# The second batch's X loads behind the third DMA transpose, and eight more identity products at the start

## The chip, the cores and the metric

The kernel runs on one core of a Trainium2 chip. The metric is the device time of one execution in microseconds (us). The engines are TensorE (PE; its weight loads are shown apart as PEld), VectorE (DVE), ScalarE (ACT), GpSimd (POOL) and SyncE (SP). SP computes nothing here: it issues DMAs, in order, and waits in front of a DMA whose source is not ready.

## The reference

One block of a speech encoder, for two batches of 4000 rows of 144 values. Cut to its core:

```
h = layernorm(x);  x = x + 0.5 * (silu(h @ w_ff1a) @ w_ff1b)       # 144 -> 576 -> 144
h = layernorm(x);  q, k, v = split(h @ w_qkv)                      # 4 heads of 36
x = x + softmax(q k^T * 36**-0.5) v @ w_o                          # all 4000 keys of the batch
h = layernorm(x);  a, b = split(h @ w_pw1);  h = a * sigmoid(b)
x = x + silu(depthwise_conv5(h, dw)) @ w_pw2
h = layernorm(x);  x = x + 0.5 * (silu(h @ w_ff2a) @ w_ff2b)
return layernorm(x)
```

## The kernel before

Rows are worked on in 16 chunks of 500, eight for each batch (CPB = 8, NCH = 16). A chunk lies in the tile X as 125 partitions by 4 blocks of 144 values. Each chunk passes two norms ahead of attention (feed-forward 1, then Q, K and V), and three after it.

A norm takes its statistics on DVE (`bn_stats`, tile ST, two instructions for a chunk), the root on POOL (tile RS), and writes normed rows into XN, on DVE, ACT or POOL. The matmuls that follow want the 144 values along the partitions, in two halves of 72. There are two ways to turn the rows:

- The first chunks of the opening (`small(c)`, chunks 0 to 3) go through PE: a product with the identity matrix (PS<-IDENT,XN in the profile) and a copy out of PSUM into XTB or XTQ.
- Later chunks go through a DMA transpose that SP issues, `dma_transp`, line 1201: XTB<-XN. For the attention norm two plain DMAs, XTQ<-XTB, follow it.

In the feed-forward part PE multiplies XTB by WA (and its remainder WE), ACT applies tanh (TH<-PS), DVE makes HT from TH and PS, and PE multiplies HT by WB. In attention PE computes scores (PS<-QT,KT), ACT or DVE their exponentials (PT<-PS), and PE multiplies these by V (PS<-PT,VA).

The kernel's text is run by a planner: every operation becomes a record with its engine, its cost and what it depends on. The planner groups the records into steps, one for each value of `R.step`. A table, ORDER, then says for each engine in which order the steps are issued, and `arrange` puts them so; two characters of a table name one step of that engine. From the records come the semaphore waits. All DMAs of SP go through one hardware queue (q1 in the profile), in SP's order.

The inputs are loaded thus: X of chunk 0 and of chunks 1 to 7 by SP, the first feed-forward weights and the QKV weights by ACT, then on SP the other weights and, in the same step as the last of them, the eight X loads of the second batch (`load_x`, 140.6 KB each). The first DMA transpose comes next on SP.

At the start PE has no rows yet. `warm` gives it products of the identity matrix by itself (PS<-IDENT, 128x128), 50 of them (NWARM) ahead of the first rows. Their result is not used. The same products also fill some gaps later on (`R.filler`).

Of the kernel before, what the change touches and what calls it, by code (L numbers as in the profile page):

```python
# [12 lines left out]
D = 144  # L13
H = 4
# [183 lines left out]
        ')o*/*#*$*)**)r*&*(*+*1*-*2*4*3*5*6*0*,*7*8'  # L198
    ),
    "pool": (  # L200
        '!!!#!$!%!&!+!(!)!*!,!-!1!B!@!/!2!4!3!.!0!5!8!9!A!:!=!6!?!<!;!7!>!D!C!E!}!G!F!J!H!I!K!L!N!t!M!O!Q!T!k'
        '!P!R!Y!S#3!U!j!W!V!`!X!Z![!]!^!f!h!_!a!b!d!g!i!c!e!l!m!n!o!u!v!w!p!y!x!z!{!r!q!|#$#!!s#&###)#(#*#%#/'
        '#1#0#2#+#-#,#.#5#6#7#8#4#;#<#=#>#Z#?#D#@#:#A#F#E#9#B#C#G#J#H#I#O#K#Q#L#M#N#S#T#P#U#V#W#X#R#^#Y#[#]#`'
        '#_#a#b#t#c#f#j#h#i#e#d#k#p#r#m#q#n#o#g#l#s#v#x#w#y#u#z$&#{#|#}$!$$$#$%$($)$*$+$,$-$/$.$0$1$2$3$4$5$6'
        '$7$>$<$=$G$?$B$@$:$A$C$E$8$D$F$M$I$K$9$H$J$N$L$;$O$Q$P$R$Y$S$W$T$X$U$[$]$Z$V$^$`$b$e$a$_$c$f$g$h$i$d'
        '$j$l$n$o$u$p$q$k$m$s$r$t$v$x$z$w%($|$y%#%!%$${%%%&%)$}%*%,%-%.%/%0%+%1%2%9%3%4%5%6%=%>%?%;%7%B%<%C%8'
        '%D%E%F%:%G%@%J%A%M%H%I%K%L'
    ),
    "sp": (
        '!!!#!$!%!&!(!)!*!+!,!-!.!/!0!1!2!4!3!5!6!8!9!;!7!<!=!>!?!A!:!@!C!D!E!F!B!G!H!I!J!K!N!P!M!L!Q!O!R!U!S'  # L210
        '!T!V!W!X!Z!Y![!_!]!^!`!d!a!e!f!g!b!h!l!i!c!j!n!m!k!o!p!q!s!t!u!r!x!v!{!y!|!z!w!}###!#$#%#&#*#(#)'
    ),
}
PLACES = (
# [92 lines left out]
def c_dve(n, rate=1.0):  # L307
    return n / (960 * rate) + 0.07
# [456 lines left out]
def bass_standalone__conformer_family_zipformer__speech_kernel(  # L765
# [13 lines left out]
    Bsz, T, Dm = x.shape  # L779
    assert Dm == D and T % CH == 0  # L780
    N = Bsz * T
# [8 lines left out]
    R = Rec(nc)  # L790
    op = R.op
    S = Sched(R)

    def sb(name, shape, dt=BF16):
        return nc.alloc_sbuf_tensor(name, [128] + list(shape), dt)
# [150 lines left out]
    ROT = 0  # L946
    SPLIT = 0
    NWARM = 50
    NPRE = 3
    KEEP = 2  # L950
    ALONE = 3
# [15 lines left out]
    X = sb("X", [NBLK, D])  # L967
# [47 lines left out]
    BX = 6  # L1015
# [22 lines left out]
    def load(eng, q, dst, src, w, r=(), lat=None):  # L1038
        op(eng, "dma_start", dst, src, q=q, r=r, w=w, cost=0.45, lat=lat)

    def kh(wap):
        return wap.rearrange("(k p) n -> p k n", p=HD)

    def load_x(eng, c, r=()):
        load(eng, f"x{c}", X[0:TB, c * NB:(c + 1) * NB, :], x_tok[c], [("X", c, i) for i in range(NB)], r, 2.9)

    def load_ff(eng, qa, qb, WA, WE, WB, wa, wb, nm, la=None, lb=None):
        load(eng, qa, WA[0:HD, :, :], kh(wa)[:, :, 0:512], [(nm, "a", 0)], lat=la)
        load(eng, qa, WE[0:HD, :, 64:128], kh(wa)[:, :, 512:FF], [(nm, "a", 1)], lat=la)
        load(eng, qb, WB[:, 0:4, :], wb[0:512, :].rearrange("(t p) d -> p t d", p=128), [(nm, "b", 0)], lat=lb)  # L1050
        load(eng, qb, WB[0:64, 4, :], wb[512:FF, :], [(nm, "b", 1)], lat=lb)
        load(eng, qb, WB[64:128, 5, :], wb[512:FF, :], [(nm, "b", 2)], lat=lb)
# [28 lines left out]
        load("sp", "w2", WP2Z[i * LC:(i + 1) * LC, i, :], w_pw2[ML:D, :], [("WP2Z", i)])  # L1081
    load("sp", "w2", DWR[0:KCONV, 0:D], dw, ["DWR"])
    load_ff("sp", "w2", "w2", WA2, WE2, WB2, w_ff2a, w_ff2b, "W2")
    for c in range(CPB, NCH):
        load_x("sp", c)

# [22 lines left out]
    def warm(cost=0.056, bk=BX + 1, n0=0):  # L1109
        op("pe", "matmul", PSV[:, bk, n0:n0 + 128], lhsT=IDENT[:, :], rhs=IDENT[:, :], start=True, stop=True, r=["ID"],  # L1110
           w=[("ps", bk)], cost=cost, kind="f")

    for i in range(NWARM):
        warm(0.1, BX + i % 2, i // 2 % 4 * 128)
    R.filler = warm
    R.filler_free = lambda: max([o.done for h in R.hist[("ps", BX + 1)] for o in h if o.eng != "pe"], default=0.0) + 0.06

# [493 lines left out]
    def pre(c):  # L1611
        if c == 0:
            yield from pre_first()
        else:
            yield from ff1(c)
            yield from pre2(c)
# [282 lines left out]
    def series(gens):  # L1899
        for g in gens:  # L1900
            yield from g
            if ROT:
                S.threads.remove(S.cur)
                S.threads.append(S.cur)
# [216 lines left out]
    for c in range(CPB):  # L2121
# [3 lines left out]
                m=c_dve(2 * CH, 2), w=c_dve(2 * CH, 4))  # L2125
# [161 lines left out]
    def pick():  # L2287
        got = pick_any()
        if mode["front"] and not stats["exp"] and not (got[1] == "T" and got[2].rank < 0):
            eng = "pe" if got[1] in "SO" else got[2].req.eng if got[1] == "T" else "act"  # L2290
            ts = [(S.start_of(th), th) for th in S.threads if th.rank < 0 and th.req.eng == eng]
            ts = [q for q in ts if q[0] is not None and q[0] < max(got[0], R.free[eng]) + FIRST]
            if ts:
                t, th = min(ts, key=lambda q: q[0] - 0.25 * q[1].req.hold + FJ[q[1].no % len(FJ)])
                return t, "T", th
        return got
# [98 lines left out]
    while n_s[0] < NIT or eq or pend or live_dve[0]:  # L2395
        seg[0] = max(seg[0], n_s[0] // SEG)
        if mode["front"] and len(kv_done) == CPB:
            mode["front"] = False
            front[:] = [0.0, n_s[0]]
            S.add(setup_dw())  # L2400
            for par in range(NPRE):
                S.add(series(pre(c) for c in range(CPB + par, NCH, NPRE)), R.last)
            for par in range(2):
# [3 lines left out]
        if due():  # L2407
            n = n_s[0]
# [13 lines left out]
        t, k, v = pick()  # L2422
        R.step += 1
        if k == "S":
            n = n_s[0]
# [15 lines left out]
    while S.threads:  # L2441
        c = [(S.start_of(th), th) for th in S.threads]
        c = [(t, th) for t, th in c if t is not None]
# [42 lines left out]
```

## Time and profile before

| | us |
|---|---|
| median of 3 runs | 880.66 |
| the three runs | 879.81, 880.66, 881.91 |
| the profiled execution | 877.03 |
| its span, first to last instruction | 875.2 |
| PE / DVE / ACT / POOL busy | 854.3 / 843.8 / 838.6 / 282.8 |

The span is 1.8 us shorter than the time of the same execution. All rows of the profile are from that execution, and their times count from the start of its span. Nearly every instruction is recorded by one helper and shows line L591, so groups are told apart by engine and tile. A row of a timeline merges neighbouring instructions of one kind (x8 is eight of them); its second number runs from the first one's start to the last one's end. For SPq that is the time of issuing, not of the transfer.

### The profile page before, as it was taken

The page shows a single profiled execution, that of the slowest core. Times are in us where ns is not written, and L with a number is a line of the kernel's source. Part 1 is how long each engine was busy: PE and PEld are TensorE (multiplying, and loading weights), DVE is VectorE, ACT ScalarE, POOL GpSimd, SP SyncE. Part 2 cuts the span into 40 slices and gives each one's busy share as a digit, 9 for nine tenths or more (in the row PEclk, how much of TensorE's full clock was granted, in tenths as well). Part 3 has the DMA queues.
Part 4 walks back from the last instruction along what each step waited for, and adds up shares of the span by engine and source line. Part 5 has one row for each costly group of instructions (what it writes and reads, how often), then busy time and mean ns, then how long its engine had stood idle before and what let it go on. Part 6 is the DMA issues. An engine that isn't in the chain of part 4 may idle for free.

```text
span 875.2 us, 27133 instructions
## 1 busy us (share of the span) xinstructions
PE 854.3 (98%) x11629; PEld 412.5 (47%) x11629; DVE 843.8 (96%) x1853; ACT 838.6 (96%) x1101; POOL 282.8 (32%) x540
## 2 busy tenths in 40 slices
PE   8999999999999999999999999999999999999996
PEld 7643444444344444444444444444545444444586
DVE  7899999999999999999999999999999999999987
ACT  7799999999999999999999999999999999999975
POOL 6670341031514302511330241210541261501645
PEclk9999999999999999999999999999999999999999
DMA  4420111102122101211310010201120021010201
GB/s 120 71 45 8 32 21 38 32 15 44 21 38 39 38 15 20 44 26 26 33 37 2 9 37 9 26 13 14 26 51 4 19 44 26 17 18 14 41 20 40
DMA packets 83552, 26.12 MB, mean 30 GB/s; under 512 B 78231, under 2 KB 83432, under 8 KB 83432
## 3 DMA queue, kind: packets, MB, share of 16 engines
q1 hardware_dynamic: 81884, 23.70, 14.8%
q8 instruction: 91, 1.49, 0.7%
q10 hardware_dynamic: 1548, 0.69, 0.3%
q14 instruction: 29, 0.24, 0.1%
HBM read 3.31 MB, written 2.30 MB: 6 GB/s over the span
## 4 chain that ended last, share of the span: by engine, by line
ACT 44%; PE 36%; DVE 16%; DMA 2%; issue 1%; POOL 1%; DVEq 0%; POOLq 0%; ACTq 0%
ACT PT L591 40%; PE PS L591 36%; DVE PT L591 10%; ACT TH L591 3%; DMA XTB<-XN 2%; DVE ST L591 1%; DVE X L591 1%; DVE U L591 1%; DVE XN L591 1%; DVE QT L591 0%; DVE HT L591 0%; DMA X<-in_x_dram 0%; DVE KT L591 0%; POOL RS L591 0%; POOL XN L591 0%
## 5 line engine op out<-in xcount | busy, mean ns | idle before, releaser
L591 ACT ACTIVATE PT<-PS 128x1000 bf16<-128x1000 f32 (+1 forms) x793 | 731.8, 1075 | 7.0 <-PE PS L591 5.5
L591 PE MATMUL PS<-QT,KT 64*64 64x500 bf16 x3968 | 455.8, 383 | 4.3 <-ACT PT L591 1.0
L591 PE MATMUL PS<-PT,VA 64*37 64x500 bf16 x4828 | 451.8, 372 | 1.8 <-DVE QT L591 0.9
L591 DVE TENSOR_SCALAR PT<-PS 128x500 int16<-128x500 f32 (+1 forms) x424 | 280.8, 680 | 4.5 <-PE PS L591 2.4
L591 PEld LDWEIGHTS PS<-QT,KT 64*64 64x64 bf16 x3968 | 138.6, 104 | 203.8 <-ACT PT L591 102.6
L591 PEld LDWEIGHTS PS<-PT,VA 64*37 64x37 bf16 x4828 | 162.9, 96 | 106.9 <-DVE PT L591 15.1
L591 POOL TENSOR_SCALAR RS<-ST 125x4 f32<-125x4 f32 (+1 forms) x118 | 31.1, 265 | 485.4 <-DVE ST L591 481.0
L591 DVE TENSOR_SCALAR PT<-PT 128x1000 uint16<-128x1000 uint16 x430 | 172.3, 418 | 1.7 <-PE PS L591 0.5
L591 DVE TENSOR_TENSOR PT<-PT 128x1000 bf16<-128x1000 bf16 x215 | 146.0, 682 | 1.1
L591 POOL TENSOR_SCALAR XN<-X,RS 125x144 bf16<-125x144 bf16 x236 | 134.6, 582 | 3.9 <-DMA out_dram<-XN 0.3
L591 POOL TENSOR_TENSOR RS<-RS,NHALF 125x4 f32<-125x4 f32 (+2 forms) x99 | 97.0, 983 | 71.8 <-DVE RS L591 69.5
L591 ACT ACTIVATE TH<-PS 128x500 bf16<-128x500 f32 (+3 forms) x175 | 95.0, 568 | 5.2 <-PE PS L591 4.5
L591 PE MATMUL PS<-XTB,WA 72*128 72x500 bf16 (+2 forms) x304 | 72.5, 344 | 3.1 <-DMA XTB<-XN 2.5
L591 DVE SCALAR_TENSOR_TENSOR HT<-TH,PS 128x500 bf16<-128x500 bf16 (+1 forms) x120 | 72.0, 617 | 3.4 <-ACT TH L591 2.4
L591 DVE BATCH_NORM_STATS2 ST<-X 125x6 f32<-125x288 bf16 (+1 forms) x160 | 66.4, 450 | 2.1 <-DMA X<-in_x_dram 1.2
L591 DVE SCALAR_TENSOR_TENSOR X<-PS,X 125x288 bf16<-125x288 f32 (+1 forms) x112 | 50.2, 452 | 4.6 <-PE PS L591 3.7
L591 PE MATMUL PS<-WB,HT 128*125 128x144 bf16 (+1 forms) x640 | 51.9, 229 | 0.1
L591 PEld LDWEIGHTS PS<-WB,HT 128*125 128x125 bf16 (+1 forms) x640 | 44.8, 136 | 12.6 <-issue 3.6
L591 PEld LDWEIGHTS PS<-XTB,WA 72*128 72x128 bf16 x304 | 22.9, 97 | 30.5 <-issue 9.0
L591 PE MATMUL PS<-U,DG 128*128 128x375 bf16 (+5 forms) x204 | 27.9, 263 | 0.1
L591 ACT ACTIVATE HT<-PS 128x500 bf16<-128x500 f32 (+3 forms) x46 | 21.4, 526 | 4.1 <-PE PS L591 3.6
L591 PE MATMUL PS<-IDF,QT 128*125 128x128 f32 x128 | 22.4, 298 | 0.0
(95 smaller groups left out, 523.0 us busy)
## 6 DMA issues: line engine op xcount, KB each, us to landing
X<-in_x_dram SPq DMA_DIRECT2D x16, 140.6 KB
XTQ<-XTB SPq DMA_DIRECT2D x24, 70.3 KB
out_dram<-XN SPq DMA_DIRECT2D x11, 140.6 KB
XTB<-XN SPq DMA_TRANSPOSE x50, 3.0
out_dram<-XN SPq DMA_DIRECT2D x6, 70.3 KB
XTB<-AN SPq DMA_TRANSPOSE x15, 3.1
out_dram<-XN ACTq DMA_DIRECT2D x3, 70.3 KB
WA<-in_w_ff1a_dram ACTq DMA_DIRECT2D x1, 144.0 KB
```

What stands on the lines that cost most here:

```text
L591: ins = getattr(eng, o.name)(*o.a, **o.k)
```

## The change

Two edits, and new order tables that number the steps anew.

- A step of their own for the eight X loads of the second batch. In SP's table this step is put behind the third DMA transpose. Before, SP issues: weights, eight X loads, four transposes. After: weights, three transposes, eight X loads, the fourth transpose.
- Eight more identity products (NMORE) behind the 50. The planner's clocks are put back to where they were ahead of them, so that they change nothing in what it plans.

On every engine the order of all else is the same, and no instruction gets a wait that it did not have.

```diff
     "sp": (
-        '!!!#!$!%!&!(!)!*!+!,!-!.!/!0!1!2!4!3!5!6!8!9!;!7!<!=!>!?!A!:!@!C!D!E!F!B!G!H!I!J!K!N!P!M!L!Q!O!R!U!S'
...
+        '!!!#!%!&!(!$!)!*!+!,!-!.!/!0!1!2!3!5!4!6!7!9!:!<!8!=!>!?!@!B!;!A!D!E!F!G!C!H!I!J!K!L!O!Q!N!M!R!P!S!V'
...
     NWARM = 50
+    NMORE = 8
...
     load_ff("sp", "w2", "w2", WA2, WE2, WB2, w_ff2a, w_ff2b, "W2")
+    R.step += 1
     for c in range(CPB, NCH):
         load_x("sp", c)
...
     def warm(cost=0.056, bk=BX + 1, n0=0):
         op("pe", "matmul", PSV[:, bk, n0:n0 + 128], lhsT=IDENT[:, :], rhs=IDENT[:, :], start=True, stop=True, r=["ID"],
            w=[("ps", bk)], cost=cost, kind="f")
+        return R.ops[-1]
 
     for i in range(NWARM):
         warm(0.1, BX + i % 2, i // 2 % 4 * 128)
+    was = dict(R.free), R.last, R.issue, list(R.quad), R.kind
+    for i in range(NMORE):
+        R.trims.append((warm(0.056, BX + i % 2, i // 2 % 4 * 128), 0.056, 0.1))
+    R.free, R.last, R.issue, R.quad, R.kind = was
```

The table of POOL changes too, only because the steps after the new one have other numbers.

More of the change, by code (lines that the diff above doesn't have):

```diff
@@ L200 @@
     "pool": (
[L201 to L207, printed above, removed]
+        '!!!#!$!%!&!(!,!)!*!+!-!.!2!C!A!0!3!5!4!/!1!6!9!:!B!;!>!7!@!=!<!8!?!E!D!F#!!H!G!K!I!J!L!M!O!u!N!P!R!U'
+        '!l!Q!S!Z!T#4!V!k!X!W!a!Y![!]!^!_!g!i!`!b!c!e!h!j!d!f!m!n!o!p!v!w!x!q!z!y!{!|!s!r!}#%##!t#(#$#*#)#+#&'
+        '#0#2#1#3#,#.#-#/#6#7#8#9#5#<#=#>#?#[#@#E#A#;#B#G#F#:#C#D#H#K#I#J#P#L#R#M#N#O#T#U#Q#V#W#X#Y#S#_#Z#]#^'
+        '#a#`#b#c#u#d#g#k#i#j#f#e#l#q#s#n#r#o#p#h#m#t#w#y#x#z#v#{$(#|#}$!$#$%$$$&$)$*$+$,$-$.$0$/$1$2$3$4$5$6'
+        '$7$8$?$=$>$H$@$C$A$;$B$D$F$9$E$G$N$J$L$:$I$K$O$M$<$P$R$Q$S$Z$T$X$U$Y$V$]$^$[$W$_$a$c$f$b$`$d$g$h$i$j'
+        '$e$k$m$o$p$v$q$r$l$n$t$s$u$w$y${$x%)$}$z%$%#%%$|%&%(%*%!%+%-%.%/%0%1%,%2%3%:%4%5%6%7%>%?%@%<%8%C%=%D'
+        '%9%E%F%G%;%H%A%K%B%N%I%J%L%M'
     ),
     "sp": (
-        '!!!#!$!%!&!(!)!*!+!,!-!.!/!0!1!2!4!3!5!6!8!9!;!7!<!=!>!?!A!:!@!C!D!E!F!B!G!H!I!J!K!N!P!M!L!Q!O!R!U!S'
-        '!T!V!W!X!Z!Y![!_!]!^!`!d!a!e!f!g!b!h!l!i!c!j!n!m!k!o!p!q!s!t!u!r!x!v!{!y!|!z!w!}###!#$#%#&#*#(#)'
+        '!!!#!%!&!(!$!)!*!+!,!-!.!/!0!1!2!3!5!4!6!7!9!:!<!8!=!>!?!@!B!;!A!D!E!F!G!C!H!I!J!K!L!O!Q!N!M!R!P!S!V'
+        '!T!U!W!X!Y![!Z!]!`!^!_!a!e!b!f!g!h!c!i!m!j!d!k!o!n!l!p!q!r!t!u!v!s!y!w!|!z!}!{!x#!#$###%#&#(#+#)#*'
     ),
```

## The prediction

> **What bounds the kernel now.** I read the page first, for the balance of the engines.
>
> ```profile
> span 875.2 us, 27133 instructions
> PE 854.3 (98%) x11629; PEld 412.5 (47%) x11629; DVE 843.8 (96%) x1853; ACT 838.6 (96%) x1101; POOL 282.8 (32%) x540
> ```
>
> Three engines are busy for 96 to 98% of the span, in an order that is written out, so a stall in the opening stage pushes everything behind it, and only there is anything left to gain. The change touches nothing but the first microseconds of PE and one stretch of SP's queue. So the chain of waits between 20 and 55 us comes next (start, length, what).
>
> ```profile
> 23.04 0.27 DVE XN L591
> 23.30 6.31 DMA XTB<-XN
> 29.62 0.05 issue
> 29.66 17.16 PE PS L591 x192
> 46.83 0.02 issue
> 46.85 1.00 ACT PT L591
> ```
>
> The first DMA transpose is a link of that chain: 6.31 us, then 17 us of matmuls without a break, then the attention stage. SP's timeline shows what stands ahead of it, and the list of DMA issues what a transpose usually takes (its last number, from issue to landing).
>
> ```profile
> 16.42 4.81 SPq L591 DMA_DIRECT2D X<-in_x_dram  x8
> 23.30 8.98 SPq L591 DMA_TRANSPOSE XTB<-XN  x2
> 35.71 1.23 SPq L591 DMA_TRANSPOSE XTB<-XN  x1
> 51.55 1.23 SPq L591 DMA_TRANSPOSE XTB<-XN  x1
> XTB<-XN SPq DMA_TRANSPOSE x50, 3.0
> X<-in_x_dram SPq DMA_DIRECT2D x16, 140.6 KB
> ```
>
> So it took 3.3 us longer than the usual 3.0. The eight X loads were all issued by 21.23, so SP was not what held the transpose; the data was. The DMA view between 20 and 40 us, in 40 slices of half a microsecond, shows it:
>
> ```profile
> DMA  3334333339933333860000004992000001993000
> GB/s 122 118 124 150 124 120 124 124 118 256 175 124 120 124 124 99 160 150 0 0 0 0 0 0 99 216 198 61 0 0 0 0 0 32 219 206 67 0 0 0
> ```
>
> A stream of about 122 GB/s runs from before 20 to about 28 us: the X loads (8 of 140.6 KB, 1.15 MB, 9.4 us at that rate). The transpose appears in two pieces, in slices 10 and 11 (24.5 to 25.5) and, when the stream ends, in slices 17 and 18 (28 to 29). The second transpose (32 to 34) and the third (36.5 to 38.5), with nothing beside them, are one piece each of under 2 us. The first is half done and then waits for the X loads.
>
> **The X loads behind the third transpose.** What the stall costs, engine by engine (timelines; in brackets the idle time before and its releaser):
>
> ```profile
> 26.64 1.44 PE L591 MATMUL PS<-XTB,WA 72*128 72x500 bf16 x6
> 29.66 0.60 PE L591 MATMUL PS<-XTB,WA 72*128 72x500 bf16 x2 [1.59 <-DMA XTB<-XN]
> 26.61 2.19 ACT L591 ACTIVATE TH<-PS 128x500 bf16<-128x500 f32 x4 [0.18 <-PE PS L591]
> 30.73 1.97 ACT L591 ACTIVATE TH<-PS 128x250 bf16<-128x250 f32 x4 [1.92 <-PE PS L591]
> 27.38 2.41 DVE L591 SCALAR_TENSOR_TENSOR HT<-TH,PS 128x500 bf16<-128x500 bf16 x4
> 31.14 0.42 DVE L591 SCALAR_TENSOR_TENSOR HT<-TH,PS 128x250 bf16<-128x250 bf16 x1 [1.34 <-ACT TH L591]
> 35.68 1.59 DVE L591 SCALAR_TENSOR_TENSOR HT<-TH,PS 128x500 bf16<-128x500 bf16 x3 [0.31 <-ACT TH L591]
> 21.42 1.85 POOL L591 TENSOR_SCALAR XN<-X,RS 125x144 bf16<-125x144 bf16 x4
> ```
>
> When is the first transpose issued? It waits for POOL, which finishes its rows at 21.42 + 1.85 = 23.27; that is unchanged, and SP, now free since 16.4, issues at 23.30 as before. With nothing ahead it lands at 23.30 + 3.0 = 26.30. What is late next is PE itself: from its rows of six and of two such matmuls a further one costs (1.44 - 0.60)/4 = 0.21 us, so the one that waits could start at 26.64 + 6 x 0.21 = 27.90, not 29.66: 1.76 earlier. The landing is then 1.6 us early, so it need not be exact. ACT is free at 28.80 and could gain up to 1.92; it follows PE. DVE is free at 29.79 and can move its next HT by only 1.34 at first. These three bound the gain, 1.34 to 1.92. I take 1.75, nearest to PE's row, because the 17.16 us behind it are a chain of PE, and DVE, 0.41 short at first, has 0.31 of idle time at 35.68 to catch up in.
>
> Then everything up to the end would move by 1.75, if nothing with a fixed time stands in the way. The next such items are the second and third transposes, and the first consumers of both on PE's load row:
>
> ```profile
> 29.23 1.79 POOL L591 TENSOR_SCALAR XN<-X,RS 125x144 bf16<-125x144 bf16 x4
> 33.01 2.67 POOL L591 TENSOR_SCALAR XN<-X,RS 125x144 bf16<-125x144 bf16 x6
> 37.69 0.58 PEld L591 LDWEIGHTS PS<-XTB,WA 72*128 72x128 bf16 x4
> 42.82 0.20 PEld L591 LDWEIGHTS PS<-XTB,WA 72*128 72x128 bf16 x2
> ```
>
> POOL, not moved by the change, ends their rows at 31.02 and 35.68, and SP issues at 31.05 (the second of the row of two: 23.30 + 8.98 - 1.24) and 35.71. They land at about 34.1 and 38.7. Their consumers, moved forward by 1.75, come at 35.94 and 41.07. Margins: 1.8 and 2.4 us. So neither stalls, provided that the third is not slowed.
>
> The eight loads themselves now start at 35.71 + 1.23 = 36.94 and hold SP for 4.81 us, to 41.75. Behind them on SP stands the fourth transpose, which waits for rows that come with the moved chain, at 51.55 - 1.75 = 49.80: 8 us after SP is free. Their data takes 9.4 us after a start-up; even with 2 us of that it has drained by 48.4, so 1.4 us are left. Who needs the X of the second batch?
>
> ```profile
> L591 DVE BATCH_NORM_STATS2 ST<-X x28: 435/448/463, 4.7 to 51.6; 125x6 f32<-125x288 bf16 x28
> 91.03 0.81 DVE L591 BATCH_NORM_STATS2 ST<-X 125x6 f32<-125x288 bf16 x2
> ```
>
> The first row is that of the tile ST up to 90 us. The first batch alone has eight chunks with two norms of two such instructions ahead of attention, 32 in all, so the 28 started by 51.6 fit into it, and the next comes at 91.03. Loads that land by 48.4 are 42 us early. Cost of the delay: nothing. Removed from 17 to 28 us is DMA traffic that no other row waits for.
>
> **Eight more identity products.** They stand behind the 50 at the start of PE's queue, with no wait of their own. The rows:
>
> ```profile
> 1.52 4.60 PE L591 MATMUL PS<-IDENT 128*128 128x128 bf16 x50 [1.52 <-POOL NHALF L591]
> 6.76 0.41 PE L591 MATMUL PS<-IDENT,XN 125*72 125x125 bf16 x4 [0.65 <-DVE XN L591]
> L591 PE MATMUL PS<-IDENT x33: 260/314/314, 1.5 to 4.9; 128*128 128x128 bf16 x33
> 10.73 0.55 PE L591 MATMUL PS<-IDENT 128*128 128x128 bf16 x7
> 11.89 0.89 PE L591 MATMUL PS<-IDENT 128*128 128x128 bf16 x13
> ```
>
> The first 33 start within 1.5 to 4.9 us, 3.4/32 = 0.106 us apart; later ones, by the rows of 13 and of 7, (0.89 - 0.55)/6 = 0.057. So here the clock doubles at about 5 us. Eight at 0.057 are 0.46 us, inside the 0.65 that PE waits for DVE's first rows: nothing on the path. If the clock were still slow, the 50 would end their starts at 1.52 + 50 x 0.106 = 6.82, already behind 6.76, and eight at 0.106 would put 0.85 us in front of the first rows. These are the bounds, nothing and 0.85; I take nothing, since the row shows the fast pitch. A gain from them (a clock that is released sooner) has no row: the release comes before they run.
>
> The Trainium skill (TensorE: Matmul & The Clock Gate, Part 1) says that the clock is released by a free-running activity window of about 3.4 us, so that the moment differs between runs. By that rule this trace (release about 3.4 us after the first product) has nearly the earliest moment, other executions pay up to the whole 0.85, and the sum would be a gain of about 0.9. One trace cannot show the spread.
>
> **The sum.** Gain 1.75 - 0 = 1.75 us. The profiled execution took 877.03 us for its span of 875.22; it would become 875.3, with a span of 873.5. The median of the runs is 880.66, 3.6 above the profiled execution, and they range from 879.81 to 881.91. I take the same difference off the median: 878.9. The bound for a difference that a measurement of this kernel can tell, 0.2%, is 1.76 us, so the forecast lies on that bound.
>
> **Rivals.**
>
> *The clock comes later.* The eight products then stand ahead of the first rows. Price: up to 0.85, deciding from the point where 58 products end after 6.76, which is a release about 0.7 us later than here (the 0.65 idle less 0.46 leaves 0.19; each microsecond of slow clock costs 0.5). Against it: the pitch in the trace. It leaves a gain of 0.9 to 1.7, or 879.0 to 879.8. I put into this case, too, that the gain is given back later to some transfer whose margin I have not seen.
>
> *The stall is longer in the timed runs.* They are 3.6 us longer than the profiled execution. If some of that is a slower X stream, the wait for the first transpose is longer by as much, and the change removes all of it: at one to two more microseconds, 877 to 878. Against it: the stream in the trace is steady at 122 GB/s.
>
> *The third transpose is caught (slower).* The first one was held half done until the X stream ended. If loads issued right behind a transpose, in the same queue, can hold it too, the third lands at the end of the drain, some 48.4 + 0.5 us, rather than 38.7. PE then waits at the weights that begin at 42.82 now, and the time grows by about 6: 887. It decides from a landing after 42.82 + 1.76 = 44.6; between 41.07 and 42.82 it only eats the gain. For it: the first transpose shows that a transpose beside X traffic can stand still. Against it: there the loads were ahead, issued from 16.42, and the third is finished by 38.5 while loads issued at 36.94 have hardly begun to move data. The change also is what it says: in the built order only the eight loads and the products move, and no wait is added.
>
> **The numbers.** Forecast 0.58, of which about half falls on either side of the bound (0.30 faster, 0.28 same), given the scatter of about 1 us in the runs; longer stall 0.20 (faster); late clock or gain given back 0.13 (same); third transpose caught 0.09 (slower). So 0.50, 0.41 and 0.09. The forecast's own range is 878.2 to 879.6 (1.34 to 1.92, and the scatter of a median); with the longer stall below, and a lost gain and scatter above, 877.4 to 881.0, which leaves out the slower case and a tenth more.
>
> **What would show it.** In the profile after: the eight X loads of SP at about 37; the first transpose still issued at 23.3 and landing 3 us later; PE's wait of 1.59 before the matmul at 29.66 gone, that matmul at 27.9; matmuls of the third transpose at about 41.1 without a wait for DMA; the attention stage, at 46.85 now, at 45.1; PE's first rows still at 6.76, with a gap of 0.2. I am wrong if the first transpose still takes over 4.5 us, if XTB appears as a releaser around 41 us, or if the first rows come after 6.9.

## The result and the profile after

| | before | after |
|---|---|---|
| median, us | 880.23 (10 runs) | 875.26 (10 runs) |
| lowest and highest | 876.65 and 882.88 | 874.88 and 875.96 |
| profiled execution: time, span | 877.03, 875.2 | 875.88, 874.0 |

The ratio is 0.9951, with a 95% interval of 0.9931 to 0.9970: faster by 5 us, where 1.75 was forecast, and outside the range given. Two numbers of the table matter more than the medians. The two profiled executions differ by 1.15 us only. And the runs of before spread over 6 us, those of after over one. Sorted, the ten runs of before are 876.65, 876.85, 877.28, 877.39, and then 879.81 to 882.88: two groups, and the profile on which the prediction rests came from the lower one.

What the change does in its own stage is what was forecast. SP's timeline after:

```profile
23.45 13.69 SPq L591 DMA_TRANSPOSE XTB<-XN  x3
37.19 4.67 SPq L591 DMA_DIRECT2D X<-in_x_dram  x8
```

The DMA view after, from 20 to 50 us in 40 slices of 0.75 us:

```profile
DMA  1000006900000000493000198133334333333200
GB/s 22 0 0 0 0 0 139 202 9 0 0 11 0 0 0 22 97 184 80 0 0 0 37 214 157 51 108 123 121 121 145 120 121 123 123 123 121 100 0 0
```

The first transpose is one piece now (slices 7 and 8, 24.5 to 26.0), and so is the third (slices 23 to 25, 36.5 to 38.75); the stream of X at about 122 GB/s follows it and has drained by 48.5. PE after, around the matmul that waited:

```profile
26.78 1.86 PE L591 MATMUL PS<-XTB,WA 72*128 72x500 bf16 x8
28.48 0.59 PE L591 MATMUL PS<-XTB,WE 72*128 72x250 bf16 x4
28.91 2.28 PE L591 MATMUL PS<-XTB,WA 72*128 72x500 bf16 x10
```

The groups of six and of two have become one of eight without a gap. The four WE products start at 28.48 rather than 30.10. The chain after has lost its DMA link:

```profile
22.77 22.44 PE PS L591 x268
45.21 0.02 issue
45.23 1.00 ACT PT L591
```

Attention starts at 45.23, 1.62 before its old place (46.85), although PE's first rows come 0.29 later:

```profile
1.52 5.69 PE L591 MATMUL PS<-IDENT 128*128 128x128 bf16 x58 [1.52 <-POOL NHALF L591]
7.05 0.39 PE L591 MATMUL PS<-IDENT,XN 125*72 125x125 bf16 x4
```

Not all of the 1.62 reaches the end: the two spans differ by 1.2. The largest loss is near 113 us. PE's load row there, after (first) and before (second):

```profile
113.19 0.55 PEld L591 LDWEIGHTS PS<-XTQ,WK 72*128 72x128 bf16 x4 [0.96 <-DMA XTQ<-XTB]
114.06 0.54 PEld L591 LDWEIGHTS PS<-XTQ,WK 72*128 72x128 bf16 x4 [0.22 <-issue]
```

The lead is down to 0.87. The transpose ahead of these XTQ transfers took 4.9 us from issue to landing in the profile after, rather than 3.0; the last section says what passed beside it. The second profile of the changed kernel has the same wait (0.95).

### The profile page after: what moved, and what is told of

It is laid out like the page before. It is cut to its first block, busy times and chain, and to the rows that moved or that the text cites. A ratio compares the mean times of both kernels' runs of the same rounds, so it can differ in the third digit from the quotient of the medians.

```text
span 874.0 us, 27149 instructions
## 1 busy us (share of the span) xinstructions
PE 855.2 (98%) x11637; PEld 413.3 (47%) x11637; DVE 843.6 (97%) x1853; ACT 839.0 (96%) x1101; POOL 283.4 (32%) x540
## 4 chain that ended last, share of the span: by engine, by line
PE 43%; ACT 38%; DVE 16%; DMA 1%; issue 1%; POOL 1%; DVEq 0%; POOLq 0%; ACTq 0%
PE PS L591 43%; ACT PT L591 35%; DVE PT L591 11%; ACT TH L591 3%; DVE ST L591 1%; DMA XTB<-XN 1%; DVE U L591 1%; DVE X L591 1%; DVE XN L591 1%; DVE HT L591 0%; DVE QT L591 0%; DVE SW L591 0%; POOL XN L591 0%; DVE AN L591 0%; ACT KT L591 0%
```

## The experiments

There are four series, each on another chip, with runs of the kernel before beside it as its base. Versions of one series compare best. All times in us.

| kernel | series | median | lowest, highest | runs |
|---|---|---|---|---|
| before (base) | 1, 2, 3, 4 | 881.55, 880.72, 881.02, 877.17 | 876.26, 886.29 | 29, 27, 15, 17 |
| X loads moved, 50 products | 1, 3 | 875.72, 875.94 | 874.98, 880.41 | 12, 7 |
| 58 products, X loads in place | 1 | 880.61 | 877.17, 884.81 | 12 |
| 26 products, X loads in place | 1 | 879.17 | 877.90, 881.61 | 10 |
| stall filled, 28 products | 2 | 875.95 | 875.00, 876.38 | 9 |
| one X load moved | 2 | 875.89 | 875.10, 881.24 | 12 |
| X loads moved, 38 products | 2 | 877.50 | 874.58, 879.24 | 12 |
| after, again | 2 | 875.64 | 874.61, 876.22 | 7 |
| stall filled, 7 wide products | 3 | 877.30 | 876.92, 877.75 | 9 |
| after, 29 products of twice the width | 3 | 875.27 | 874.64, 876.45 | 6 |
| after, PE held | 4 | 881.81 | 877.19, 887.96 | 12 |

**Each half of the change alone.** The changed kernel without the eight products, and the kernel before with them:

```diff
-    NMORE = 8
+    NMORE = 0
```

> The changed kernel with NMORE = 0: only the X loads are moved. Theory A (the products decide when the TensorE clock is released; with 50 of them PE stands idle or half busy ahead of the first rows, and in some executions the release is put off by a whole further stretch): the runs fall into two groups as those of the kernel before do (876.7 to 877.4 and 879.8 to 882.9), each about 1.7 lower: 875.0 to 875.7 and 878 to 881; median 878 to 879 if the shares are as before. Theory B (the moved X loads alone remove the long runs, since in those the X stream was slower): all runs between 874.5 and 876, ratio as for the whole change, 0.995.

> The kernel before with the eight more identity products, X loads left in their place. Theory A: one group only, about 1.7 above the changed kernel, 876.5 to 878; ratio to before 0.996 to 0.998 by medians, and the stall before the matmul that waits for the first DMA transpose stays (about 1.6 us of PE). Theory B: two groups as before, median 880 plus 0 to 0.5.

Measured: the X loads alone give 875.72, ratio 0.9943 (0.9923 to 0.9962), the whole gain. The products alone give 880.61 with runs from 877.17 to 884.81, ratio 0.9989 (0.9965 to 1.0013): both groups are still there. Theory A falls. Theory B said the right thing of the runs, but for two of the twelve with the X loads moved (876.46 and 880.41, where it allowed up to 876), and was still to be tested for its reason.

**The kernel before, once more.**

> The kernel before, unchanged, profiled once more: which group it falls into is open. If it is the upper one (over 879), theory A expects the difference to arise before 15 us, with a later rise of the product rate on PE; theory B expects it between 23 and 30 us, in the wait for the first DMA transpose.

It took 880.70: a run of the upper group, with a profile. Neither theory placed the difference rightly. The wait for the first transpose is the same as in the lower group, 1.63 against 1.59, and the X stream runs at 120 to 124 GB/s as there. What differs comes behind it. PE in this run (first fence) and in the first profile of before (second):

```profile
26.91 1.44 PE L591 MATMUL PS<-XTB,WA 72*128 72x500 bf16 x6
29.97 0.60 PE L591 MATMUL PS<-XTB,WA 72*128 72x500 bf16 x2 [1.63 <-DMA XTB<-XN]
30.84 3.80 PE L591 MATMUL PS<-XTB,WA 72*128 72x500 bf16 x10
34.57 3.10 PE L591 MATMUL PS<-PT,VA 64*37 64x500 bf16 x26
```

```profile
30.53 2.28 PE L591 MATMUL PS<-XTB,WA 72*128 72x500 bf16 x10
32.74 1.65 PE L591 MATMUL PS<-PT,VA 64*37 64x500 bf16 x26
```

The same ten matmuls take 3.80 rather than 2.28, the same 26 take 3.10 rather than 1.65. TensorE runs at half its clock. The windows view shows where that starts and ends (columns: stretch, length, busy time of PE, PEld, DVE, ACT and POOL with the number of instructions, then PEclk, the granted clock, with 1.00 for full speed, and last the busy share of DMA and its GB/s):

```profile
28.00:31.41 3.41, 1.78 (x11) 0.89 (x10) 2.07 (x4) 1.45 (x4) 3.41 (x8) 1.00 0.27 63
31.42:34.83 3.41, 3.41 (x13) 1.05 (x14) 2.51 (x5) 1.91 (x4) 3.22 (x7) 0.50 0.41 79
34.83:38.23 3.40, 3.40 (x28) 1.08 (x21) 1.84 (x3) 2.17 (x5) 1.12 (x3) 0.50 0.36 70
38.25:41.66 3.41, 3.41 (x41) 2.88 (x40) 2.32 (x5) 2.30 (x5) 0.00 (x0) 1.00 0.05 11
```

The clock record of the trace changes at 31.42 and 38.25: 6.83 us at half clock. By 39 us this run is 3.3 us further behind the first profile than it was at 24 us (3.57 against 0.27), and it keeps that to the end. The borders are no accident. In every trace here the distances between changes are multiples of 3.41 us: 23.89 (seven) from the first release to the halving, 6.83 (two), 10.2 (three) or 13.65 (four) at half clock. So there is a grid of 3.41 us, and it sits elsewhere in each execution; the clock is first released at 7.52 in this run and at 4.97 in the first profile. In the first profile the stall lies between about 28.1 and 29.7, and the grid gives:

```profile
25.45:28.86 3.41, 2.62 (x22) 1.46 (x21) 3.19 (x8) 3.12 (x5) 3.27 (x6) 1.00 0.48 134
28.87:32.27 3.40, 2.61 (x15) 1.42 (x16) 1.91 (x5) 1.50 (x4) 3.40 (x8) 1.00 0.01 1
```

A border cut the stall in halves there, PE was busy for 77% of both stretches, and the clock stayed. In the other run the stall (about 28.3 to 30.0) lay in one stretch, 52% busy, and the next two ran at half clock. The version with 58 products and X in place agrees, from a third position of the grid (1.99 of 3.41 is 58%):

```profile
26.81:30.22 3.41, 1.99 (x13) 0.81 (x11) 3.11 (x6) 2.10 (x4) 3.27 (x8) 1.00 0.34 85
30.23:37.04 6.81, 6.81 (x35) 2.54 (x36) 3.74 (x8) 3.98 (x9) 5.42 (x12) 0.50 0.21 42
```

This became theory C: the stall costs its own time, and, where the grid does not cut it, a halved clock worth some 3.3 to 3.6 us more, about half of the 6.83 us.

**The stall filled.** If so, a stall that stays but is filled with unused products must cost only itself. The edit puts them in front of the matmul that waits, with no wait of their own:

```diff
+    fill = next(o for o in R.ops if o.eng == "pe" and any(d.name == "dma_start_transpose" for d, raw in o.deps))
...
+    for i in range(NFILL):
+        op("pe", "matmul", PSV[:, BX + 1, i % 4 * 128:i % 4 * 128 + 128], lhsT=IDENT[:, :], rhs=IDENT[:, :], start=True,
```

> The kernel before, X loads in their old place and 50 products at the start, with 28 unused identity products put into PE's stall, right before the matmul that waits for the first DMA transpose (28 x 0.056 = 1.57 us, inside the 1.59 of idle time). Theory C (the stall costs twice: its own 1.6 us, and, where it falls into one activity window of 3.4 us, a TensorE clock halved for 6.83 us, worth 3.6): the stall stays, the clock is kept, so nearly all runs between 876.5 and 878, ratio to before about 0.995, and no stretch of clock 0.5 near 30 us. Theory B (in the long runs the X stream is slower): filling cannot help, the runs spread from 876.6 to 884 as before, ratio 1.000.

```profile
28.06 1.73 PE L591 MATMUL PS<-IDENT 128*128 128x128 bf16 x28
29.73 0.60 PE L591 MATMUL PS<-XTB,WA 72*128 72x500 bf16 x2
```

The upper group is gone: nine runs from 875.00 to 876.38. The matmul still starts at 29.73, as late as ever. But the median, 875.95, is below the 876.5 to 878 that theory C allowed, and only 0.3 above that of the changed kernel in the same series. Either the stall's own cost is given back later, or the 28 products did something else. The next version keeps the stall and the clock and adds 7 wide products in their place (WA by itself, 512 columns):

> The kernel before with the stall filled again, by 7 unused products of 512 columns (WA by itself, 7 x 0.21 = 1.5 us) rather than by 28 of 128: the same stall kept and the same clock kept, but 42 fewer PE instructions added. Theory E (the stall's own 1.6 us stay in the total; the version with 28 products was quick, at 875.95, because the extra instructions moved PE's instruction refills away from late transposes): one group at 876.6 to 877.6, ratio to before 0.996. Theory F (the stall's own cost is given back later; only the clock costs): 875.0 to 876.4 again, ratio 0.994.

```profile
27.99 1.67 PE L591 MATMUL PS<-WA 72*128 72x512 bf16 x7
30.34 0.60 PE L591 MATMUL PS<-XTB,WA 72*128 72x500 bf16 x2 [0.68 <-DMA XTB<-XN]
26.90:30.31 3.41, 2.76 (x13) 1.07 (x11) 2.98 (x6) 1.93 (x4) 3.27 (x9) 1.00 0.41 113
```

One group, 876.92 to 877.75, where the lower group of before lies, and 1.4 to 2.0 above the two versions without the stall in the same series (875.94 and 875.27). The stall was 2.3 us long in this profile, filled part included. So here most of the stall's own cost stays in the total, as theory E has it, and the clock's is the rest. But the stall is not simply carried to the end. The four WE products behind it start at 28.48 in the profile after, at 30.17 with 28 products and at 30.78 with 7 wide ones, so 1.69 and 2.30 later; at the end the spans are 0.1 shorter and 1.2 us longer. The rest is made up at later waits, which theory E foretold for the 28 products; the last section shows the largest of them.

**One X load moved.** Seven loads ahead of the transposes, one behind the third:

```diff
-    R.step += 1
-    for c in range(CPB, NCH):
+    for c in range(CPB, NCH - 1):
         load_x("sp", c)
+    R.step += 1
+    load_x("sp", NCH - 1)
```

> The changed kernel with only the last of the eight X loads behind the third transpose; seven stay ahead. The X stream ends 1.2 us sooner, so the first transpose lands at about 28.4 and PE's stall shrinks from 1.6 to about 0.4 us. Theory C: 0.4 us cannot halve the clock, so one group, 0.4 to 0.6 above the changed kernel: 875.5 to 876.7. If the clock is halved by any stall there, or if the long runs come from the X stream beside the opening's matmuls, a group at 879 to 881 stays.

```profile
28.67 0.60 PE L591 MATMUL PS<-XTB,WA 72*128 72x500 bf16 x2 [0.48 <-DMA XTB<-XN]
26.70:30.11 3.41, 2.93 (x19) 1.43 (x18) 3.17 (x7) 2.51 (x5) 3.27 (x8) 1.00 0.28 66
832.25:835.65 3.40, 2.27 (x17) 1.51 (x17) 2.25 (x8) 2.25 (x6) 2.35 (x4) 1.00 0.04 13
835.67:845.89 10.22, 10.22 (x72) 8.60 (x70) 4.88 (x16) 5.14 (x13) 1.09 (x5) 0.50 0.00 0
```

Eleven of twelve runs are at 875.10 to 876.11: a stall of 0.48 leaves the stretch 86% busy and the clock whole. The twelfth, 881.24, is the profiled one, and the last two rows explain it: the halving struck at 835.67, after a stretch that PE's waits near the end had left 67% busy. The profile after has such a wait too (1.20 near 833), but in its stretches of the grid PE was 88 and 85% busy there, and none of the 17 runs of the changed kernel so far was a long one.

**Fewer products at the start.** 26 with the X loads in place, and 38 with them moved:

```diff
     for i in range(NWARM):
         warm(0.1, BX + i % 2, i // 2 % 4 * 128)
+    gone = {id(o) for o in R.ops[-NLESS:]}
+    R.ops[:] = [o for o in R.ops if id(o) not in gone]
```

> The kernel before with 26 identity products at the start rather than 50, X loads left in place. Theory A: PE falls idle at about 4.3 us, ahead of the release, so the clock is released late in every execution; all runs in the upper group or above it, 880 to 884, and the granted clock in the profile starts later than 7 us. Theory B: the products do not matter for the two groups; median 880 with the same scatter.

> The changed kernel with 38 identity products at the start rather than 58. The idle time ahead of the first rows grows to over 1.1 us. Theory C: in most executions an activity window now holds that gap whole and the clock is halved for 6.83 us from about 8 us on; runs in two groups, one at 875 to 876 and most at 877 to 881. If the number of products at the start does not matter (theory D), all runs between 874.9 and 876.5.

With 26, all runs lie at 877.90 to 881.61, mostly below the 880 to 884 of theory A. In the profile the clock is granted at 4.36, earlier than theory A expected, and halved at 7.77, after a stretch in which PE was 21% busy. That opening is so slow that SP issues the first transpose at 26.54 only; the X stream ends near 28 us, about when the data of this transpose start to move, and the stall at 29 us does not occur. The long opening takes its place. With 38 there are two groups, five runs at 874.58 to 875.32 and seven at 877.05 to 879.24. The profiled run is of the upper one:

```profile
7.08 0.41 PE L591 MATMUL PS<-IDENT,XN 125*72 125x125 bf16 x4 [1.89 <-DVE XN L591]
4.45:7.86 3.41, 1.42 (x22) 1.07 (x20) 2.40 (x9) 1.46 (x4) 1.39 (x2) 1.00 0.36 88
7.87:14.68 6.81, 6.81 (x46) 5.71 (x46) 2.75 (x12) 4.63 (x8) 2.02 (x3) 0.50 0.51 144
```

So the number of products can matter in the same way: 1.89 us of idle time ahead of the first rows, a stretch 42% busy, then 6.81 us at half clock.

**The changed kernel again, and 50 products again.**

> The changed kernel again, to see whether it has a rare upper group as its version with 50 products had (one run of 12 at 880.41). Theory C: none, all within 874.8 to 876.5, since the eight products fill the gap ahead of the first rows. Theory D (the products have no effect): about one run in ten near 880.

> The version with the X loads moved and 50 products, again, for the share of its long runs: theory C (the gap ahead of the first rows can halve the clock if a window begins right with the release) about one run in ten near 879 to 880.5; theory D (products without effect) the share of the changed kernel, none in 17 so far. With 12 more runs this separates them only if two or more long ones come.

After: seven runs, 874.61 to 876.22, none high in 17 with the first ten. With 50 products: 875.33 to 877.82; with the first twelve, one run of 19 at 880.41 and one at 877.82. For the opening, the worst position of the grid that was seen in the changed kernel is this one, right behind the release:

```profile
4.27:7.68 3.41, 2.53 (x42) 2.19 (x40) 2.31 (x9) 1.63 (x4) 1.39 (x2) 1.00 0.40 96
```

74% busy, and no halving. Without the eight products (0.45 us) it would be about 61%, an estimate from this row; that is between the 58% and 67% that were halved, but also among the 59 to 66% that were not (last section). So a protection by the eight products in a few executions is possible, but two runs of 19 against none of 17 do not show it.

**Held by another engine.** The last test turns the argument round: the changed kernel, with no X load near, and that matmul made to wait for DVE instead.

```diff
+    held = next(o for o in lines["pe"] if any(d.name == "dma_start_transpose" for d, raw in o.deps))
+    held.deps.append((lines["dve"][HELD], True))
```

> The changed kernel (X loads behind the third transpose, 58 products) with PE held on purpose where the kernel before waits for the first transpose: that matmul also waits for the fourth HT of DVE before it, which ends at about 29.9 us, so PE is idle for some 1.7 us and no X load is under way. Theory C (any idle time of that size here halves the clock whenever it falls mainly into one window of 3.41 us): the runs look like those of the kernel before, a smaller group at 876.6 to 877.8 and most at 879.5 to 883; ratio to before 0.998 to 1.002. Theory B (the long runs come from the X stream): one group at 876.6 to 877.8, the stall's own 1.7 us and no more.

```profile
29.95 0.70 PE L591 MATMUL PS<-XTB,WA 72*128 72x500 bf16 x2 [1.87 <-DVE HT L591]
26.88:30.28 3.40, 1.53 (x8) 0.60 (x7) 2.92 (x6) 1.88 (x4) 3.27 (x9) 1.00 0.01 2
30.30:43.93 13.63, 13.63 (x72) 6.72 (x70) 6.59 (x12) 6.43 (x14) 5.25 (x11) 0.50 0.35 86
```

Two runs at 877.19 and 877.76, two more at 878.63 and 879.26, the rest from 880.89 to 887.96, and in the profile a halved clock, this time for four stretches of the grid. With DMA nearly silent in the stretch (2 GB/s) the long runs are back. Theory B falls; idle time of PE in this stretch is the cause, whatever makes it. The ratio, 1.0036 (1.0012 to 1.0060), says little by itself: of the 17 runs of before in series 4 ten were in the lower group (up to 877.68; median of all 877.17), against none of 15 in series 3. The median of before moves by 4 us with the share of its groups; whether the chip has a part in that share is not known, as each series ran on one of its own.

## Why the prediction was right or wrong

**The stage was read rightly, the way to the end less so.** The issue at 23.3 (23.45, since the opening came a little later), the landing 3 us on, the gapless restart of PE, the X loads at 37, the third transpose untouched, X in time, attention at 45.1 (45.23): each came as worked out. The gain of 1.75 at the restart was 1.62 at attention, with PE as what is late next. Against the lower group of before, about 877.1, the changed kernel's 875.3 to 875.6 is 1.5 to 1.8 lower. That is the whole of what the prediction counted. In the profiles themselves only 1.2 of the 1.62 arrive: that a gain could be "given back later to some transfer whose margin I have not seen" stands in the first rival, and near 113 us 0.75 us were given back, of which later waits returned a part.

**The step that failed** is the sentence of the sum that takes "the same difference off the median". It carried the 3.6 us by which the median lay above the profiled execution unchanged into the forecast. Those 3.6 were the second price of the very stall that the change removes: the halved clock of the majority of executions. The profile at hand was of an execution without it; its row of 1.59 us of idle time was priced at its own length, which holds for an execution in which the clock stays, as in this one, where the grid cut the stall. With the halved clock the same stall cost some 3.3 to 3.6 us more, and the change takes both prices away: 5 us between the medians.

**The rival that pointed there** was the second, a longer stall in the timed runs, 877 to 878, at 0.20. Its direction and its evidence, the distance of 3.6 us, were right; its mechanism was wrong, the stall in a long run being 1.63 and the X stream the same. And its price was too small. It was the only case that treated the gap between profile and median as something to be explained.

**The eight products.** "Nothing on the path" held. In the profile after, the release came at 6.34, later than in the first profile, as the clock rival had it, and the first rows at 7.05, past the 6.9 that was set as a sign of error. But DVE's first XN was itself 0.15 later there, and the version with 50 products has its first rows at 7.00. The rival *the clock comes later* thus happened, at a price that no median shows. Here the rule of the Trainium skill cited in the prediction (TensorE: Matmul & The Clock Gate, Part 1: a free-running window) is borne out: releases were seen from 4.27 to 7.52. The first profile's 4.97 was not "nearly the earliest moment". Used for the opening alone, it missed the larger use, that the same window can take the clock back in mid-kernel.

**The slower rival** did not occur; the third transpose, with the first load issued at 37.19, right behind the 37.14 at which its own issue ended, was not held. In this kernel the loads behind a transpose did not stop it, those ahead did.

## What to carry to other kernels

Price an idle stretch of PE twice: by its length, and by what it does to the clock; here 1.6 us of waiting cost 1.6 in some executions and about 5 in most. When the runs of a kernel fall into groups, find out which group the profile at hand is from, and look for the row that makes the difference, before taking a term of the sum from it. Where such a wait cannot be removed, unused products in it kept the clock here, and moving bulk loads behind the small transfer that PE waits for removed it at no cost in its own stage.

## What the runs showed of the hardware that was not expected

**The clock can be taken back after much less than an idle stretch.** Stretches of the 3.41 us grid in which PE was busy for 21, 42, 45, 52, 58 and 67% were followed by a halved clock; stretches with 74, 77, 81 and 86% were not. There is no clean border between them. Three other stretches kept the clock: 59% busy (the version with products of twice the width, 820.05 to 823.47, with a wait of 1.39 us for XTB in it), 65% (38 products, 823.65 to 827.06) and 66% (26 products, 823.56 to 826.97). So PE's busy share in such a stretch, as the profile gives it, does not decide alone, and what else does was not found. The Trainium skill (TensorE: Matmul & The Clock Gate, the table "Why this matters for your kernels") advises against idle gaps over about 3 us; here 1.6 us in the wrong place was enough, and the measurement decides. The time at half clock was two stretches in four traces, three and four in one each, although PE was busy throughout. What ends it earlier or later was not found.

**An instruction refill beside a DMA transpose can make it longer.** Queue q8, "instruction" in the profile, moves 91 packets of 16 KB, one for about 256 of PE's products and weight loads; a packet is called a refill here. From the packets of the traces: transposes with no refill under way end a median of 2.6 us after their issue, those with one take up to 3.7 to 4.2, by trace. The DMA view after, from 711 to 717 us (slices of 0.15), with SP's issue at 712.02, and PE's row:

```profile
DMA  0000000000000079999950000000399900000000
q8 instruction: 1, 0.02, 1.4%
716.37 0.11 PEld L591 LDWEIGHTS PS<-XTB,WP 72*128 72x128 bf16 x2 [1.01 <-DMA XTB<-XN]
```

The transpose stands still in its middle for about 1.2 us, beside one refill (713.16 to 714.56), and PE waits 1.01 us for it. The wait near 113 us is of this kind: the transpose issued at 104.89 has a refill beside its last packets (107.75 to 108.67) in the profile after; in the first profile of before the refill comes at 109.87, when the transpose has landed.

Adding PE instructions, or moving PE's work in time, moves the refills. With 28 products in the stall PE's load row waits for transposes for 1.1 us in all, stall filled; with 7 wide ones 3.8, the first 1.17 of them in the stall; in the profile after 3.7, and 1.0 more for XTQ. The largest difference is near 833 us. After, 28 products, and 7 wide ones:

```profile
832.87 0.33 PEld L591 LDWEIGHTS PS<-XTB,WE 72*128 72x128 bf16 x4 [1.20 <-DMA XTB<-XN]
832.65 0.42 PEld L591 LDWEIGHTS PS<-XTB,WE 72*128 72x128 bf16 x4
834.06 0.33 PEld L591 LDWEIGHTS PS<-XTB,WE 72*128 72x128 bf16 x4 [1.15 <-DMA XTB<-XN]
```

At the weights near 823 the two filled versions are 0.28 apart, here 1.41; their spans differ by 1.4. So most of that difference arises at this one wait. In the profile after and with 7 wide products a refill begins 2.6 and 2.5 us behind the issue of the transpose that PE waits for here (830.72 behind 828.11, 831.90 behind 829.36); with 28 products the refill has passed by 828.59, and the transpose issued at 829.11 is in time. So in that version no refill falls on this transpose. A direct trial, the changed kernel with its opening products made half as many and twice as wide:

> The changed kernel with its 58 identity products replaced by 29 of twice the width: the same busy time at the start, 58 fewer PE instructions ahead of everything. Theory E: the refills fall elsewhere, so the late waits of PE for transposes (near 113, 717 and 833 us, together about 3 us of the profile after) change their places or lengths, and the time moves by 0.3 to 1 us, either way, in one group. Theory F: the same late waits, 874.9 to 876.2 as the changed kernel.

```profile
PEld PS L591 <- DMA XTB<-XN: 4.2, 3, 1.7
```

The waits did change places: the one for XTQ near 113 us is gone, and one of 1.7 us has come at 823. The median, 875.27, lies between those of the changed kernel, 875.26 and 875.64. So the waits move with the instruction count, as expected, but the sum hardly does. No version was faster than the changed kernel beyond its scatter.
